# One attention and two mixture layers in one program: the first head's queries in one piece, the weight splits of MoE 1 placed and ordered anew, the weight split of MoE 2 moved behind the second group's rows

## The chip, the core and the metric

The program runs on one core of a Trainium2 chip. The core has a matmul engine (TensorE, PE in the profile, with PEld for its weight loads), a vector engine (VectorE, DVE), an activation engine (ScalarE, ACT), GpSimd (POOL), and SyncE (SP), which here only issues DMAs. Each engine runs its own list of instructions in the order written, and waits at an instruction until what it needs is done. The metric is the device time of one execution in microseconds (us). Before the change it is 1084.62 us, the median of three runs (1084.51 to 1084.77).

## The reference, cut to what matters

```python
# 1. attention: q is pooled by pairs of positions (1152 -> 576), 4 batches of 8 heads, head size 64
q_pool = q.reshape(B, H, S // 2, 2, D).mean(axis=3)
scores = scale * q_pool @ k.T
attn = exp(scores - max(scores)); attn = attn / sum(attn)
x = (attn @ v).transpose(0, 2, 1, 3).reshape(2304, 512)
# 2. MoE 1, in truth one dense layer pair
h = x @ w_in                                   # 512 -> 2048
g = where(h > 0, h, exp(min(h, 0)) - 1)
x = g @ w_out                                  # 2048 -> 512
# 3. MoE 2: a row is skipped or goes to one of 8 experts (512 -> 1024 -> 512)
do = x @ w_skip > 0; e = argmax(x @ w_gate); p = softmax(x @ w_gate)[e]
out = where(do, x + p * (maximum(x @ w1[e], 0) @ w2[e]), x)
```

## The kernel before, in words

A float32 operand that must be multiplied nearly exactly is split: a high part (`hi`, rounded to the fast matmul type by ACT) and a low part (`lo`, the rest, by a subtraction on DVE or POOL). A product then is three matmuls: high by high, high by low, low by high.

**Attention** (lines 25 to 273) goes through 16 pairs of heads. A pair has nine units of 128 queries against 1152 keys (one unit has 64 queries of either head). For a unit PE makes scores in a large piece `s2` (768 keys, two buffers) and a small one `s1` (384 keys, one buffer); DVE finds the maximum (L122, L128, L130), ACT takes the exponential (`ex`, L137 and L138) into a tile `p` of the pool `pp` (three buffers), PE transposes `p` in three groups (L165), DVE and ACT copy these out (`PT`, L169, L170), and PE multiplies by v (L180). The order in which a unit's steps are issued is the string `order='TSeTqsdTvr'`. For the very first pair the queries and keys are prepared apart, in `first(j)` (L193 to 210): `hi` and `lo` split the keys, `add` sums the two positions of a query on POOL and DVE (L200), then come the cast `qh` (L205 or L67) and the rest `ql` (L206 or L71). The first head's queries come in two pieces, 256 columns and 320; the second piece's work (`late`, L220) is issued behind the first unit's exponential and the second head's preparation (L243).

**MoE 1** (lines 319 to 404) runs over nine blocks `b` of 256 rows and 16 chunks `f` of 128 inner columns. `stage1(b,f)` is twelve matmuls (L357), then ACT's exponential (L361), two DVE instructions that make `e` (L362, L363; the second one frees the PSUM buffer `ph`, of which there are two), ACT's high part `gh` (L365) and DVE's low part `gl` (L367). `stage2(b,f)` is six matmuls (L375), two chunks behind. In block 0 `load` also brings two weight tiles a chunk (`rawi`, `rawo`, five raw buffers) and splits them on ACT (L337) and DVE (L338) at once. The first split tiles come from the pool `ip`, which takes over memory that the attention's tiles held: a tile there waits until their last readers are done.

**MoE 2** (lines 596 to 794) treats the largest expert's first two groups of rows, "a" and "b", ahead of the rest. Its weights `w1` are used as they are, `w2` is split (L639, L640) into `w2hi`, `w2lo`. `turn` transposes a group's gathered rows `xg` on PE (L646) and copies them out on ACT or DVE (L647, L648) into `xt`; `layer1` is the first product (L656) with its ReLU and split `hh`, `hl` (L658, L659); `second` is the second product (L675): sixteen matmuls with `w2hi`, then eight with `w2lo`, `py`. The group (0,0) follows "b".

Of the kernel before, what the change touches and what calls it, by code (L numbers as in the profile page):

```python
# [11 lines left out]
F32 = mybir.dt.float32  # L12
BF16 = mybir.dt.bfloat16
F32R = mybir.dt.float32r
I32 = mybir.dt.int32
U32 = mybir.dt.uint32
AF = mybir.ActivationFunctionType
ALU = mybir.AluOpType
# [3 lines left out]
P = 128  # L22


def attention(ctx,tc,qT,kT,vt,xT,ident,dram,side=None,init=None,nside=1.25,order='TSeTqsdTvr',evac=(1, 0, 0),LAG=2,TP=3,KB=1,KH=1,VW=6,LW=7,RD=1,V0=0.0,D0=5,PLAN={4: ['k', 'aK'], 5: ['as', 'bK'], 6: ['aq', 'bs', 'aQ'], 7: ['bq', 'bQ', 't']},EX=1,WARM=24):
    nc=tc.nc
    B,H,D,S=kT.shape
    SQ=S//2; NC=S//P
    SC=1.0/16.0
    pp=ctx.enter_context(tc.tile_pool(name="pp",bufs=LAG+1))  # L30
    kp=ctx.enter_context(tc.tile_pool(name="kp",bufs=2))
# [16 lines left out]
    def load_q(pr,j):  # L48
        b,hp=divmod(pr,H//2)
        qr=state[pr]["qr"][j]=kp.tile([P,2,SQ],F32,tag=f"qr{j}",name=f"qr{pr}_{j}",bufs=1)  # L50
        src=qT[b,2*hp+j].rearrange("f d n -> d f n")
        for c in ((slice(0,256),slice(256,SQ)) if pr==j==0 else (slice(0,SQ),)):
            for r in range(2): nc.sync.dma_start(qr[r*64:r*64+64,:,c],src[:,:,c])
    def load_v(pr):
        b,hp=divmod(pr,H//2)
        for j in range(2):
# [42 lines left out]
    NU=len(units)  # L99
    S3=S//3  # L100
# [31 lines left out]
    def ex(i):  # L132
        d=cur[i]; nm=d["nm"]; key,_,n=place(d["u"])
        if key not in sums: sums[key]=sp.tile([P,5,2],F32,tag="a2",name="a2_%d_%d"%key)
        a2=sums[key]
        pt=pp.tile([P,S],F32,tag="p",name="p"+nm)
        nc.scalar.activation(pt[:,2*S3:],d["s1"][:,0,:S3],AF.Exp,bias=d["nb"],scale=SC,accum_out=a2[:,n,1:2])  # L137
        nc.scalar.activation(pt[:,:2*S3].rearrange("p (c s) -> p c s",c=2),d["s2"][:,:,:S3],AF.Exp,bias=d["nb"],scale=SC,accum_out=a2[:,n,0:1])  # L138
        d["pt"]=pt
# [47 lines left out]
    V=nc.vector; G=nc.gpsimd  # L187
# [5 lines left out]
    def first(j):  # L193
        st=state[0]; r=slice(64*j,64*j+64); o=slice(64-64*j,128-64*j); ks=st["ks"][j]; kr=st["kr"]
        def hi(x,y): nc.scalar.activation(ks[r,x:y],kr[r,x:y],AF.Copy)
        def lo(x,y): V.tensor_tensor(out=ks[o,x:y],in0=kr[r,x:y],in1=ks[r,x:y].bitcast(F32),op=ALU.subtract)
        def add(c=slice(0,SQ)):
            qs=st["qs"][j]=st["qs"][j] or kp.tile([P,SQ],F32,tag=f"qs{j}",name=f"qs0_{j}",bufs=1)
            for h,e in ((slice(0,64),G),(slice(64,128),(V,G)[j])):
                e.tensor_tensor(out=qs[h,c],in0=st["qr"][j][h,0,c],in1=st["qr"][j][h,1,c],op=ALU.add)  # L200
        if j==0:

            qh=st["qh"][0]=kp.tile([P,SQ],F32R,tag="qh0",name="qh0_0"); ql=st["ql"][0]=kp.tile([P,SQ],F32R,tag="ql0",name="ql0_0")
            def q(c):
                add(c); nc.scalar.activation(qh[:,c],st["qs"][0][:,c],AF.Copy)  # L205
                V.tensor_tensor(out=ql[:,c],in0=st["qs"][0][:,c],in1=qh[:,c].bitcast(F32),op=ALU.subtract)  # L206
            hi(0,2*S3); lo(0,2*S3); q(slice(0,256)); hi(2*S3,S); lo(2*S3,S)
            return lambda: q(slice(256,SQ))
        else:
            hi(0,S); add(); lo(0,S); q_hi(0,j); q_lo(0,j,G)  # L210
    def others():
        for j in range(2):
            r=slice(64*j,64*j+64); o=slice(64-64*j,128-64*j)
            copy(state[0]["kh"],state[0]["ks"][j],r); copy(state[0]["kl"],state[0]["ks"][j],o)
        q_tail(0)
        load_v(0)
        load_k(1); load_q(1,0); load_q(1,1)
        if side: side.pop(0)()
        if init: init()
    late=first(0)  # L220
    PL={"as":lambda p:q_sum(p,0,G),"bs":lambda p:q_sum(p,1,G),"k":k_hi,"t":q_tail,"aq":lambda p:q_hi(p,0),"bq":lambda p:q_hi(p,1),
        "aK":lambda p:k_lo(p,0,G),"bK":lambda p:k_lo(p,1,G),"aQ":lambda p:q_lo(p,0,G),"bQ":lambda p:q_lo(p,1,G)}
    last={(u[0],u[1]//2):i for i,u in enumerate(units) if u[1] in (1,3) and u[2]==1}
# [2 lines left out]
    for i in range(NU+LAG+8):  # L226
        k=i-LAG; w=i%9
        nxt=i<NU and units[i][0]+1<NPR
        pr=i//9
        if nxt:  # L230
            if pr+2<NPR:
                if w==LW: load_k(pr+2)
                if w==LW+1: load_q(pr+2,0)
        if w==0 and 1<=pr and pr+1<NPR and i<NU: load_q(pr+1,1)
        if nxt:
            if w==VW: load_v(pr+1)
        credit+=rate
        nv=min(len(pend),int(credit)) if i<NU else len(pend)
        credit-=nv
        nvs=order.count("v"); g=0; vi=0  # L240
        for o in order:
            if o=="r" and i==0:
                ex(0); first(1); late(); others()  # L243
            if o=="S":
                if i<NU: s_big(i)
            elif o=="e":
                if 1<=i-EX<NU: ex(i-EX)
                while kept: kept.pop(0)()
            elif o=="q":
                while after: after.pop(0)()  # L250
                if nxt:
                    for x in PLAN.get(w,()): PL[x](pr+1)
            elif o=="s":
                if i<NU: s_small(i)
            elif o=="v":
                for _ in range((nv*(vi+1)+nvs-1)//nvs-(nv*vi+nvs-1)//nvs):
                    if pend: pend.pop(0)()
                vi+=1
            elif o=="T":
                if 0<=k<NU: transpose(k,g)  # L260
                g+=1
            elif o=="r":
                if i-RD in ends: rinv(ends[i-RD])
            elif o=="d":
                if side and D0<=i<NU:
                    sc+=nside
                    while sc>=1 and side: side.pop(0)(); sc-=1
        if 0<=k<NU:
            cur.pop(k)
            if k in ends:  # L270
                assert not pend
                rows(ends[k]); pend+=pv_parts(ends[k]); rate=(9/4 if ends[k][1]==0 else 9/5)+.01; credit=V0
# [46 lines left out]
def moe1(ctx,tc,xp,rp,xT,w_in,w_out,on_pair,R,TB=256,LAGF=2,raw=None,XF=(13,6),EXTRA=(3,5,7,9,11,13)):  # L319
    nc=tc.nc  # L320
# [3 lines left out]
    ip=ctx.enter_context(tc.tile_pool(name="ip",bufs=1))  # L324
    wp=ctx.enter_context(tc.tile_pool(name="wp",bufs=1))
    gp=ctx.enter_context(tc.tile_pool(name="gp",bufs=3))
    psH=ctx.enter_context(tc.tile_pool(name="psH",bufs=2,space=PSUM))
    psX=ctx.enter_context(tc.tile_pool(name="psX",bufs=2*NTT,space=PSUM))
    wih=[];wil=[];woh=[];wol=[]
    wi_v=w_in.rearrange("(k p) f -> p k f",p=P); wo_v=w_out.rearrange("(k p) e -> p k e",p=P)  # L330
    def load(kind,f):
        shape=[P,KC,P] if kind=="i" else [P,DM]
        r=rp.tile(shape,F32,tag="raw",name=f"raw{kind}{f}")
        pool=ip if f<(3 if kind=="i" else 1) else wp
        hi=pool.tile(shape,F32R,name=f"w{kind}h{f}"); lo=pool.tile(shape,F32R,name=f"w{kind}l{f}")
        nc.sync.dma_start(r,wi_v[:,:,f*P:(f+1)*P] if kind=="i" else wo_v[:,f])
        nc.scalar.activation(hi,r,AF.Copy)  # L337
        nc.vector.tensor_tensor(out=lo,in0=r,in1=hi.bitcast(F32),op=ALU.subtract)  # L338
        (wih if kind=="i" else woh).append(hi); (wil if kind=="i" else wol).append(lo)
    xs={}  # L340
    def xsplit(b):
# [8 lines left out]
    def stage1(b,f):  # L350
        xh,xl=xs[b]
        ph=psH.tile([P,512],F32,tag="ph",name=f"ph{b}_{f}")
        wh,wl=wih[f],wil[f]
        n=0
        for cc in range(KC):
            for w,x in ((wh,xh),(wh,xl),(wl,xh)):
                nc.tensor.matmul(ph[:,:TB],w[:,cc],x[:,cc],start=(n==0),stop=(n==3*KC-1)); n+=1  # L357
        if b==0 and f+2<KF: load("i",f+2)
        if b==0 and f+1<KF: load("o",f+1)
        e=gp.tile([P,TB],F32,tag="e",name=f"e{b}_{f}",bufs=2)  # L360
        nc.scalar.activation(e,ph[:,:TB],AF.Exp)  # L361
        nc.vector.tensor_scalar(out=e,in0=e,scalar1=1.0,scalar2=-1.0,op0=ALU.min,op1=ALU.add)  # L362
        nc.vector.scalar_tensor_tensor(out=e,in0=ph[:,:TB],scalar=0.0,in1=e,op0=ALU.max,op1=ALU.add)  # L363
        gh=gp.tile([P,TB],F32R,tag="gh",name=f"gh{b}_{f}"); gl=gp.tile([P,TB],F32R,tag="gl",name=f"gl{b}_{f}")
        nc.scalar.activation(gh,e,AF.Copy)  # L365
        mid()
        nc.vector.tensor_tensor(out=gl,in0=e,in1=gh.bitcast(F32),op=ALU.subtract)  # L367
        G[(b,f)]=(gh,gl)
# [17 lines left out]
    q=[]; todo=[]; mids=[]  # L386
    def mid():
        if mids and next(mids[0])=="after": todo.append(mids.pop(0))
# [207 lines left out]
class Experts:  # L596
# [117 lines left out]
    def run(s,steps,psL):  # L714
        tc,nc,r=s.tc,s.nc,s.r; E=r.E
        with ExitStack() as c:
# [4 lines left out]
            for _ in range(3):  # L721
                next(steps); next(la)
            next(steps)
            s.split(0,"hi")
            for _ in la: pass
            s.turn("b",3,"b",e=nc.vector)
            next(lb)
            for _ in steps:
                next(lb); next(lb)
# [12 lines left out]
            def turn(k,j,e=None):  # L742
                x=s.at[k,j]=len(s.at)%4; s.turn((k,j),x,f"{k}_{j}",e=e)
            i=2
# [13 lines left out]
                    next(fews[k])  # L758
                return go
            s.layer2(0,s.lta[:,0],"a","a",ha,0)  # L760
            turn(0,0)
            s.layer2(0,s.lta[:,1],"b","b",hb,1)
            tile(0,0,{7:[lambda: turn(0,1)]})
            tile(0,1,{7:[lambda: (turn(3,0),turn(1,2,nc.vector))]},{1:[lambda: turn(1,0)]})
            s.load(4,ee[4])
# [108 lines left out]
```

## Time and profile before

| what | value |
|---|---|
| median of three runs | 1084.62 us |
| the profiled execution | 1084.87 us, its span 1083.2 us |
| PE busy | 1044.2 us, 96% of the span |
| DVE, ACT, POOL busy | 738.6, 589.0, 320.0 us |
| mean granted TensorE clock | 0.991 of 2.4 GHz |

The profiled execution lasts 1.67 us longer than its span. Its time is within 0.25 us of the median. A timeline row is: start in us, duration in us, engine, source line, operation, what is written and read, how many instructions are merged (xN); in brackets the idle time of the engine just before the row, and what ended it.

### The profile page before, as it was taken

To read this page: it belongs to the slowest core of one execution; us is meant where nothing else is said; L and a number is where in the kernel's file an instruction comes from. 1 tells how busy PE (TensorE), PEld (TensorE's weight loads), DVE (VectorE), ACT (ScalarE), POOL (GpSimd) and SP (SyncE) were. 2 spreads that over 40 slices of the span, in tenths; PEclk is the share of its full clock that TensorE was granted. 3 is DMA by queue.
4 is the path that set the end of the run, shared out by engine and by line. 5 is a ranking of instruction groups with operands and counts; after the bars stand their busy time and mean duration, and the time that the engine had idled before them with its cause. 6 is when DMAs were issued, how large, how long until landed. Compare 5 with 4: busy or idle time off the path is not lost. (4 is left out here: it accounts for less than half of the span.)

```text
span 1083.2 us, 20229 instructions
## 1 busy us (share of the span) xinstructions
PE 1044.2 (96%) x7435; PEld 852.5 (79%) x7435; DVE 738.6 (68%) x1887; ACT 589.0 (54%) x1365; POOL 320.0 (30%) x500
## 2 busy tenths in 40 slices
PE   6999999999999999999999999999999999999995
PEld 5677776777767766777688999999999998888884
DVE  4788877887878887876577646778777675542331
ACT  4888787887778877887554323333333333220230
POOL 4565445666445665443000000000000000114111
PEclk8999999999999999999999999999999999999998
DMA  8765556765566664553074010110101101338960
GB/s 209 197 166 161 145 152 168 190 188 145 152 157 178 190 177 137 153 145 95 4 201 145 22 40 21 40 39 2 40 1 40 38 3 40 110 106 307 400 221 11
DMA packets 66156, 133.56 MB, mean 123 GB/s; under 512 B 9212, under 2 KB 18940, under 8 KB 66048
## 3 DMA queue, kind: packets, MB, share of 16 engines
q1 hardware_dynamic: 63904, 127.44, 40.0%
q0 software_dynamic: 2144, 4.75, 1.4%
q8 instruction: 60, 0.98, 0.4%
q14 instruction: 48, 0.39, 0.1%
HBM read 93.37 MB, written 20.17 MB: 105 GB/s over the span
## 5 line engine op out<-in xcount | busy, mean ns | idle before, releaser
L165 PE MATMUL t<-ident,p 128*128 128x128 f32 x1152 | 197.5, 281 | 8.5 <-ACT PT L170 7.9
L165 PEld LDWEIGHTS t<-ident,p 128*128 128x128 f32 x1152 | 137.7, 141 | 70.0 <-ACT PT L170 27.9
L170 ACT ACTIVATE PT<-t 128x384 f32<-128x384 f32 x288 | 140.0, 492 | 62.2 <-PE t L165 58.1
L180 PE MATMUL o<-PT,v 128*64 128x256 f32 (+1 forms) x1152 | 170.3, 418 | 0.0
L357 PE MATMUL ph<-xh,wih 128*128 128x256 f32 x576 | 163.4, 284 | 2.0 <-DVE e L363 1.2
L357 PE MATMUL ph<-xl,wih 128*128 128x256 f32 x576 | 162.1, 282 | 0.0
L357 PE MATMUL ph<-xh,wil 128*128 128x256 f32 x576 | 161.1, 280 | 0.2 <-DVE wil L338 0.2
L534 POOL DMA_INDIRECT rowlist<-meta,sl x18 | 18.8, 1042 | 431.9 <-DVE sl L533 248.7
L115 PE MATMUL s<-ks,qh 128*128 128x384 f32 x384 | 130.5, 394 | 8.9 <-ACT p L137 5.3
L122 DVE TENSOR_REDUCE m<-s 128x1 f32<-128x768 f32 x128 | 122.4, 956 | 15.7
L365 ACT ACTIVATE gh<-e 128x256 fp32r<-128x256 f32 x144 | 60.2, 418 | 130.6 <-DVE e L363 130.6
L85 POOL TENSOR_TENSOR kl<-kr,kh 64x288 fp32r<-64x288 f32 x120 | 97.1, 839 | 96.8 <-ACT kh L81 89.8
L361 ACT ACTIVATE e<-ph 128x256 f32<-128x256 f32 x144 | 55.0, 382 | 129.5 <-PE ph L357 129.5
L357 PEld LDWEIGHTS ph<-xh,wih 128*128 128x128 f32 x576 | 108.2, 188 | 12.8 <-issue 6.0
L138 ACT ACTIVATE p<-s,nb 128x768 f32<-128x768 f32 x128 | 115.1, 899 | 0.0
L375 PE MATMUL px<-woh,gh 128*128 128x512 f32 x288 | 114.9, 399 | 0.0
L169 DVE COPY PT<-t 128x384 f32<-128x384 f32 x144 | 79.5, 552 | 51.1 <-PE t L165 49.4
L375 PE MATMUL px<-wol,gh 128*128 128x512 f32 x288 | 113.6, 395 | 0.0
L180 PEld LDWEIGHTS o<-PT,v 128*64 128x64 f32 x1152 | 70.3, 136 | 53.3 <-issue 22.3
L357 PEld LDWEIGHTS ph<-xl,wih 128*128 128x128 f32 x576 | 108.3, 188 | 5.0
L375 PE MATMUL px<-woh,gl 128*128 128x512 f32 x288 | 112.2, 389 | 0.0
L115 PE MATMUL s<-ks,ql 128*128 128x384 f32 x384 | 109.4, 339 | 0.0
(258 smaller groups left out, 1943.0 us busy)
## 6 DMA issues: line engine op xcount, KB each, us to landing
qr<-qT SPq DMA_DIRECT2D x62, 288.0 KB, 7.6
w<-w SPq DMA_DIRECT2D x16, 1024.0 KB, 13.8
v<-vt SPq DMA_DIRECT2D x32, 288.0 KB, 3.3
kr<-kT SPq DMA_DIRECT2D x15, 576.0 KB, 6.5
ks<-kh SPq DMA_DIRECT2D x30, 288.0 KB, 3.9
ks<-kl SPq DMA_DIRECT2D x30, 288.0 KB, 3.4
d<-w_in SPq DMA_DIRECT2D x16, 512.0 KB, 5.2
d<-w_out SPq DMA_DIRECT2D x16, 512.0 KB, 4.2
```

The source lines that it names most:

```text
L85: for c in range(0,S,S//4): e.tensor_tensor(out=st["kl"][o,c:c+S//4],in0=st["kr"][r,c:c+S//4],in1=st["kh"][r,c:c+S//4].bitcast(F32),op=ALU ...
L115: nc.tensor.matmul(dst[:,ci,:S3],st[n][j][:,t*P:t*P+P],st["ks"][j][:,c*S3:c*S3+S3],start=first,stop=last)
L122: nc.vector.tensor_reduce(out=m2[:,0:1],in_=s2[:,:,:S3],op=ALU.max,axis=AX.XY)
L138: nc.scalar.activation(pt[:,:2*S3].rearrange("p (c s) -> p c s",c=2),d["s2"][:,:,:S3],AF.Exp,bias=d["nb"],scale=SC,accum_out=a2[:,n,0:1])
L165: nc.tensor.transpose(po[:,c],pt[:,(g*3+c)*P:(g*3+c+1)*P],ident)
L169: if evac[g]: nc.vector.tensor_copy(o,s)
L170: else: nc.scalar.activation(o,s,AF.Copy)
L180: nc.tensor.matmul(cell["o"][64*a:64*a+64,:n],state[pr]["v"][a][:,c],src[:,c,a,:n],start=(c==0),stop=(c==NC-1))
L357: nc.tensor.matmul(ph[:,:TB],w[:,cc],x[:,cc],start=(n==0),stop=(n==3*KC-1)); n+=1
L361: nc.scalar.activation(e,ph[:,:TB],AF.Exp)
L365: nc.scalar.activation(gh,e,AF.Copy)
L375: nc.tensor.matmul(X[b][t][:,:DM],a[:,t*P:(t+1)*P],w,start=(f==0 and i==0),stop=(f==KF-1 and i==2))
```

## The change

Lines of the changed program are numbered some 2 to 10 lower than those of before, since lines went away.

```diff
     def load_q(pr,j):
-        src=qT[b,2*hp+j].rearrange("f d n -> d f n")
-        for c in ((slice(0,256),slice(256,SQ)) if pr==j==0 else (slice(0,SQ),)):
-            for r in range(2): nc.sync.dma_start(qr[r*64:r*64+64,:,c],src[:,:,c])
+        for r in range(2): nc.sync.dma_start(qr[r*64:r*64+64],qT[b,2*hp+j].rearrange("f d n -> d f n"))
...
-            hi(0,2*S3); lo(0,2*S3); q(slice(0,256)); hi(2*S3,S); lo(2*S3,S)
-            return lambda: q(slice(256,SQ))
+            hi(0,2*S3); lo(0,2*S3); hi(2*S3,S); add(); q_hi(0,j); q_lo(0,j,V); lo(2*S3,S)
...
-            if o=="r" and i==0:
-                ex(0); first(1); late(); others()
+            if o=="r" and i==0: first(1); others()
...
-                if 1<=i-EX<NU: ex(i-EX)
+                if 0<=i-EX<NU: ex(i-EX)
...
-        pool=ip if f<(3 if kind=="i" else 1) else wp
+        pool=ip if f<(2 if kind=="i" else 1) else wp
...
         nc.scalar.activation(hi,r,AF.Copy)
-        nc.vector.tensor_tensor(out=lo,in0=r,in1=hi.bitcast(F32),op=ALU.subtract)
+        def low(): nc.vector.tensor_tensor(out=lo,in0=r,in1=hi.bitcast(F32),op=ALU.subtract)
+        if kind=="i" or f==0: low()
+        else: lows.append(low)
...
         nc.scalar.activation(gh,e,AF.Copy)
+        while lows: lows.pop(0)()
...
+            for _ in la: pass
+            s.turn("b",3,"b")
             s.split(0,"hi")
-            for _ in la: pass
-            s.turn("b",3,"b",e=nc.vector)
...
-            turn(0,0)
-            s.layer2(0,s.lta[:,1],"b","b",hb,1)
+            for n,_ in enumerate(s.second(0,s.lta[:,1],"b","b",hb,1)):
+                if n: turn(0,0)
```

Where the instructions stand now is shown by three pieces of the built programs. At the program's start on ACT, before (`ks` are the first pair's keys, `qh` the queries' high parts of head 0 and 1, `p` the exponentials, `s` the scores):

```order
L195 ACTIVATE ks_0_155<-kr_116 64x768
L205 ACTIVATE qh_0_157<-qs_0_161 128x256
L195 ACTIVATE ks_0_155<-kr_116 64x384
L137 ACTIVATE p_0_0_182,a_0_0_181<-s_0_0_175,nb_0_0_179 128x384
L138 ACTIVATE p_0_0_182,a_0_0_181<-s_0_0_168,nb_0_0_179 128x768
L195 ACTIVATE ks_1_156<-kr_116 64x1152
L67 ACTIVATE qh_1_190<-qs_1_186 128x576
L205 ACTIVATE qh_0_157<-qs_0_161 128x320
L137 ACTIVATE p_1_0_303,a_0_0_181<-s_1_0_284,nb_1_0_288 128x384
```

And in the changed program:

```order
L193 ACTIVATE ks_0_153<-kr_116 64x768
L193 ACTIVATE ks_0_153<-kr_116 64x384
L65 ACTIVATE qh_0_161<-qs_0_158 128x576
L193 ACTIVATE ks_1_154<-kr_116 64x1152
L65 ACTIVATE qh_1_185<-qs_1_181 128x576
L135 ACTIVATE p_0_0_276,a_0_0_275<-s_0_0_174,nb_0_0_178 128x384
L136 ACTIVATE p_0_0_276,a_0_0_275<-s_0_0_167,nb_0_0_178 128x768
L135 ACTIVATE p_1_0_298,a_0_0_275<-s_1_0_279,nb_1_0_283 128x384
```

The first unit's exponential stands behind both heads' casts now, and the second unit's exponential right behind it, where the late piece of head 0 stood.

On DVE from the last product of the attention into MoE 1's first chunks, before (`xT` is that product, `wil` and `wol` are low parts of weights, `e` and `gl` those of the chunk's inner values):

```order
L185 TENSOR_TENSOR xT<-o_1_6989,bc_1_6987 128x256
L338 TENSOR_TENSOR wil_7054<-rawi_7052,wih_7053 128x512
L338 TENSOR_TENSOR wil_7060<-rawi_7058,wih_7059 128x512
L338 TENSOR_TENSOR wol_7066<-rawo_7064,woh_7065 128x512
L338 TENSOR_TENSOR wil_7085<-rawi_7083,wih_7084 128x512
L338 TENSOR_TENSOR wol_7091<-rawo_7089,woh_7090 128x512
L362 TENSOR_SCALAR e_0_7095<-e_0_7095 128x256
L363 SCALAR_TENSOR_TENSOR e_0_7095<-ph_0_7070,e_0_7095 128x256
L367 TENSOR_TENSOR gl_0_7100<-e_0_7095,gh_0_7099 128x256
```

And in the changed program:

```order
L329 TENSOR_TENSOR wil_7049<-rawi_7047,wih_7048 128x512
L329 TENSOR_TENSOR wil_7055<-rawi_7053,wih_7054 128x512
L329 TENSOR_TENSOR wol_7061<-rawo_7059,woh_7060 128x512
L183 TENSOR_TENSOR xT<-o_1_6984,bc_1_6982 128x256
L329 TENSOR_TENSOR wil_7080<-rawi_7078,wih_7079 128x512
L355 TENSOR_SCALAR e_0_7089<-e_0_7089 128x256
L356 SCALAR_TENSOR_TENSOR e_0_7089<-ph_0_7065,e_0_7089 128x256
L329 TENSOR_TENSOR wol_7086<-rawo_7084,woh_7085 128x512
L361 TENSOR_TENSOR gl_0_7094<-e_0_7089,gh_0_7093 128x256
```

Three splits went ahead of the attention's last product, and the `wol` of each chunk from ahead of the two instructions on `e` to behind them, ahead of `gl`.

On ACT in MoE 2, before (`ex` belongs to the router, `hha` and `hhb` are the inner values of groups "a" and "b", `pt` holds transposed rows):

```order
L504 ACTIVATE ex_11999<-d_11993 128x16
L639 ACTIVATE w2hi_11907<-xT 128x2048
L639 ACTIVATE w2hi_11908<-xT 128x2048
L658 ACTIVATE hha<-pha_11963 128x512
L658 ACTIVATE hha<-pha_12026 128x512
L658 ACTIVATE hhb<-phb_12053 128x512
```

And in the changed program:

```order
L498 ACTIVATE ex_11994<-d_11988 128x16
L652 ACTIVATE hha<-pha_11958 128x512
L652 ACTIVATE hha<-pha_12019 128x512
L642 ACTIVATE xt_11898<-ptb 128x512
L633 ACTIVATE w2hi_11902<-xT 128x2048
L633 ACTIVATE w2hi_11903<-xT 128x2048
L652 ACTIVATE hhb<-phb_12048 128x512
```

The two wide splits moved behind group "a"'s inner values and group "b"'s transposed rows, whose copy was on DVE. On PE the four transpositions of group (0,0) moved from ahead of group "b"'s second product to behind its sixteenth matmul.

## Rows read from the trace of the kernel before

**Rows 1.** Busy time by stretches: us, then engines; last granted clock, DMA, GB/s
```profile
15.88:26.12 10.24, 6.41 (x25) 5.71 (x24) 5.65 (x10) 4.83 (x12) 6.41 (x53) 0.50 1.03 272
30.00:530.00 500.00, 490.99 (x3550) 363.44 (x3550) 394.57 (x824) 401.50 (x950) 262.54 (x394) 1.00 0.57 155
590.00:952.00 362.00, 361.82 (x2350) 327.37 (x2349) 246.08 (x858) 115.02 (x279) 17.93 (x18) 1.00 0.11 39
```

**Rows 2.** Timeline of the first 22 us, from the first unit's exponential on
```profile
10.38 2.87 POOL L200 TENSOR_TENSOR qs<-qr 64x576 f32<-64x576 f32 x2 [4.41 <-DMA qr<-qT]
10.68 0.58 ACT L137 ACTIVATE p<-s,nb 128x384 f32<-128x384 f32 x1 [2.52 <-DVE nb L130]
...
11.40 0.44 PE L115 MATMUL s<-ks,qh 128*128 128x384 f32 x1 [1.24 <-ACT p L137]
...
13.44 0.68 ACT L67 ACTIVATE qh<-qs 128x576 fp32r<-128x576 f32 x1
...
14.20 2.27 POOL L71 TENSOR_TENSOR ql<-qs,qh 128x288 fp32r<-128x288 f32 x2 [0.95 <-ACT qh L67]
...
14.84 0.98 DVE L200 TENSOR_TENSOR qs<-qr 64x320 f32<-64x320 f32 x1
...
17.82 0.49 DVE L206 TENSOR_TENSOR ql<-qs,qh 128x320 fp32r<-128x320 f32 x1 [2.00 <-ACT qh L205]
...
19.10 0.55 DVE L128 TENSOR_REDUCE m<-s 128x1 f32<-128x384 f32 x1
...
20.71 0.69 PE L115 MATMUL s<-ks,qh 128*128 128x384 f32 x1 [3.83 <-ACT p L137]
```

**Rows 3.** Timeline from the attention's end into MoE 1's first chunks
```profile
538.70 1.15 ACT L337 ACTIVATE wih<-rawi 128x512 fp32r<-128x512 f32 x2 [3.62 <-PE o L180]
...
539.38 0.38 PE L357 MATMUL ph<-xh,wih 128*128 128x256 f32 x1 [0.85 <-ACT wih L337]
...
543.27 0.36 PE L357 MATMUL ph<-xh,wih 128*128 128x256 f32 x1 [0.30 <-DVE e L363]
```

**Rows 4.** Timeline of one late chunk of block 0, from `gh` on
```profile
578.72 0.42 ACT L365 ACTIVATE gh<-e 128x256 fp32r<-128x256 f32 x1 [1.23 <-DVE e L363]
...
580.09 0.36 ACT L361 ACTIVATE e<-ph 128x256 f32<-128x256 f32 x1
...
580.31 0.68 DVE L338 TENSOR_TENSOR wol<-rawo,woh 128x512 fp32r<-128x512 f32 x1
...
580.91 0.28 DVE L362 TENSOR_SCALAR e<-e 128x256 f32<-128x256 f32 x1
...
581.80 0.36 PE L357 MATMUL ph<-xh,wih 128*128 128x256 f32 x1
```

**Rows 5.** Timeline of PE: first chunk of block 1, and two later chunks
```profile
585.72 0.36 PE L357 MATMUL ph<-xh,wih 128*128 128x256 f32 x1 [0.89 <-DVE e L363]
...
591.42 0.28 PE L357 MATMUL ph<-xh,wih 128*128 128x256 f32 x1
...
594.22 0.28 PE L357 MATMUL ph<-xh,wih 128*128 128x256 f32 x1
```

**Rows 6.** Timeline of MoE 2's groups "a" and "b"
```profile
958.39 3.70 ACT L639 ACTIVATE w2hi<-xT 128x2048 fp32r<-128x2048 f32 x2
...
962.22 0.60 PE L646 MATMUL ptb<-ident,xgb 128*128 128x128 f32 x4
...
963.80 0.68 DVE L647 COPY xt<-ptb 128x512 f32<-128x512 f32 x1
...
964.54 1.16 PE L656 MATMUL phb<-xt,xT 128*128 128x128 f32 x8 [1.72 <-DVE xt L647]
...
979.59 0.66 PE L646 MATMUL pt<-ident,xg 128*128 128x128 f32 x4 [1.56 <-DMA xg<-x2d,lt]
...
980.35 0.60 ACT L648 ACTIVATE xt<-pt 128x512 f32<-128x512 f32 x1 [7.26 <-PE pt L646]
...
983.81 2.03 PE L675 MATMUL pyb<-w2lo,hhb 128*128 128x512 f32 x8
```

More of the change, by code (lines that the diff above doesn't have):

```diff
@@ L196, in lo, with add @@
         def lo(x,y): V.tensor_tensor(out=ks[o,x:y],in0=kr[r,x:y],in1=ks[r,x:y].bitcast(F32),op=ALU.subtract)
-        def add(c=slice(0,SQ)):
-            qs=st["qs"][j]=st["qs"][j] or kp.tile([P,SQ],F32,tag=f"qs{j}",name=f"qs0_{j}",bufs=1)
+        def add():
+            qs=st["qs"][j]=kp.tile([P,SQ],F32,tag=f"qs{j}",name=f"qs0_{j}",bufs=1)
             for h,e in ((slice(0,64),G),(slice(64,128),(V,G)[j])):
-                e.tensor_tensor(out=qs[h,c],in0=st["qr"][j][h,0,c],in1=st["qr"][j][h,1,c],op=ALU.add)
+                e.tensor_tensor(out=qs[h],in0=st["qr"][j][h,0],in1=st["qr"][j][h,1],op=ALU.add)
         if j==0:
[L203 to L206, printed above, removed]
-            hi(0,2*S3); lo(0,2*S3); q(slice(0,256)); hi(2*S3,S); lo(2*S3,S)
-            return lambda: q(slice(256,SQ))
+            hi(0,2*S3); lo(0,2*S3); hi(2*S3,S); add(); q_hi(0,j); q_lo(0,j,V); lo(2*S3,S)
         else:
@@ L219, in others @@
         if init: init()
-    late=first(0)
+    first(0)
     PL={"as":lambda p:q_sum(p,0,G),"bs":lambda p:q_sum(p,1,G),"k":k_hi,"t":q_tail,"aq":lambda p:q_hi(p,0),"bq":lambda p:q_hi(p,1),
@@ L328, in moe1 @@
     psX=ctx.enter_context(tc.tile_pool(name="psX",bufs=2*NTT,space=PSUM))
-    wih=[];wil=[];woh=[];wol=[]
+    wih=[];wil=[];woh=[];wol=[];lows=[]
     wi_v=w_in.rearrange("(k p) f -> p k f",p=P); wo_v=w_out.rearrange("(k p) e -> p k e",p=P)
```

## The prediction

> **What bounds the kernel now.** I read the busy times by stretches first. In the attention PE is busy 490.99 of 500 us, in MoE 1 after its first block 361.82 of 362 [rows 1]: there nothing but PE's own work counts, and no part of the change takes a matmul away. So I went to the places where PE stands idle, and read each with the engine named as the one that ended the wait. Three of them touch the change. At the start PE waits 3.83 us for an exponential [rows 2]; from the attention's end through block 0 of MoE 1 it waits again and again for ACT and DVE [rows 3 to 5]; at MoE 2's beginning it waits 1.72 us for a copy and 1.56 us for gathered rows [rows 6]. Behind each place PE is the bound again, so what PE wins or loses there should reach the end. An idle time of another engine, such as ACT's 7.26 us [rows 6], is worth nothing by itself.
>
> **Part 1, the start.** Before, the second unit's maximum on DVE (19.10) stands behind `ql` of head 0's late piece (17.82), for which DVE waited 2.00 us: `ql` needs the cast `qh`, that the addition on POOL, and POOL did head 1's `ql` first (14.20, 2.27 us) [rows 2]. With one piece this chain is gone. What is late next is the first unit's exponential, now behind both casts. POOL's additions for head 1 end at 10.38 + 2.87 = 13.25; the cast begins at 13.44 and takes 0.68, so the exponential begins at 14.12 in place of 10.68, 3.44 later. PE's next scores followed it by 11.40 − 10.68 = 0.72: 14.84. They take 0.44; the maximum can follow at once, at about 15.3, and from a maximum to the scores that waited for its exponential it was 20.71 − 19.10 = 1.61: these can start at 16.9 in place of 20.71. But PE has the third unit's products and two groups of transpositions to do between. Before, its list from 11.40 was done at 20.71 − 3.83 = 16.88, that is in 5.48 us with the waits in it; with all of that they start at 20.3, so between 16.9 and 20.3. I take the middle, 18.6: 2.1 us earlier. That stretch runs at a granted clock of 0.50, up to 26.12 [rows 1]. If the clock rises at the same time as before, the work done early is worth half, 1.05; if it rises as much earlier, all 2.1. I take **−1.5**.
>
> The bounds: at best the whole idle time goes, −3.8. At worst the wait only moves to another place and the larger additions come on top. One of 64x576 takes POOL 2.87 / 2 = 1.44, which PE then loses at half clock (0.7) or in full: about +1.0. What hides them: POOL stood idle 4.41 us ahead of head 1's additions, waiting for the load [rows 2]; without that cover they cost the 1.44. SP issues two loads fewer, POOL one addition fewer, and `others` comes a little earlier; I cost these at nothing, beside the loads.
>
> The addition of 320 columns on DVE at 14.84, while POOL's subtraction ran, took 0.98 us; DVE's subtraction of as many columns at 17.82, with POOL silent, took 0.49 [rows 2]. The Trainium skill ("SBUF — State Buffer", section "SBUF: two separate sides") says that DVE, with two operands from SBUF, and GpSimd, reading SBUF, take turns at one port pair and the loser blocks for a whole instruction. The pair of rows agrees. By it head 0's two additions, now of 576 columns, would run one behind the other, and if the first scores are on the path they come later by the shorter one, about 0.49 x 576 / 320 = 0.88; at half clock that is 0.44, the start −1.1 and the whole 1076.1. I keep the sum above, since the first exponential now waits for the casts and not for these scores.
>
> **Part 2, MoE 1.** First its beginning. PE waits 0.85 us for `wih`, the first high part, and ACT had waited 3.62 us for the attention's last product [rows 3]: not for the data, but for the memory. In the changed order three DVE splits stand ahead of that product's normalisation, since the first tiles now take the exponentials' memory, which is free once the last transpositions are done; ACT's 3.62 us have room for the three casts of about 0.6 and DVE had nothing to do there either. Then PE goes on at 539.38 − 0.85 = 538.53. The third chunk started at 543.27. It can't before two chunks' first products are done, 2.80 us (a period of 2.80 in a later block [rows 5] is a `stage1` and a `stage2`, with as many columns each): 541.3; the second weight pair still comes late, I take 541.5, **−1.75**. The bounds of this step: −0.85 (only the first wait goes) and −1.95.
>
> Then the chunks of block 0. From the third chunk to the sixteenth it was (581.80 − 543.27) / 13 = 2.964 us each [rows 3, 4], though PE needs 2.80 [rows 5]. The row of chunk 15 shows a ring over ACT and DVE: the exponential is done at 580.45, but DVE is in `wol` (580.31, 0.68 us) and takes the minimum at 580.91 [rows 4]. In the changed order `wol` stands behind the two instructions on `e`. It gives back up to 580.91 − 580.31 = 0.60 from the ring, which then takes 2.37, less than 2.80. A second ring, `gh` to exponential (580.09 − 578.72 = 1.37), exponential to minimum (0.36 and about 0.05 for the hand-over) and minimum to the next `gh` (578.72 + 2.964 − 580.91 = 0.78) is 2.56, still below. So PE's 2.80 sets the period: 13 x 0.164 = 2.1 less, and chunk 15 starts at 541.5 + 13 x 2.80 = 577.9. At block 1, PE waited 0.89 and the first chunk came 585.72 − 581.80 = 3.92 after the last one [rows 4, 5]; with DVE no longer behind, 2.80: 580.7. That is 585.72 − 580.7 = 5.0 in all; I take **−4.9**. Bounds: −1.7 (the period and the wait at block 1 stay) and −5.0.
>
> What could use it up: `gl` comes 0.68 later in each chunk, behind `wol`, but its matmuls stand two chunks behind. A raw buffer is freed later by about 0.9, so the loads come later; the five of them cover that, as no row of the stretch has PE, ACT or DVE waiting for such a load. If they didn't, the period would stay near 2.96, which is the lower bound.
>
> **Part 3, MoE 2.** Before, ACT is in the two `w2hi` splits from 958.39 to 962.09, then makes group "a"'s inner values, and DVE copies group "b"'s rows at 963.80, 1.58 after PE transposed them (962.22). PE waits 1.72 [rows 6]. Now ACT copies them itself, with the splits behind. Where ACT did such a copy without a queue ahead, it began 980.35 − 979.59 = 0.76 after the transposition and took 0.60; with 0.06 for the hand-over, as from DVE's copy to PE (964.54 − 963.80 − 0.68), PE starts at 962.22 + 1.42 = 963.64: **−0.9**. The splits then end 3.70 after about 963.4, at 967.1; they are read by the second products, behind group "b"'s first one, sixty-four matmuls of which eight take about 1.1, so not ahead of some 8 us after 963.64: nothing is late. Then the transposition of group (0,0) waited 1.56 for gathered rows. It goes behind sixteen matmuls, which took about 983.81 − 979.59 − 0.60 = 3.6: the rows are there, and its copy on ACT lies beside the eight `w2lo` products of 2.03 [rows 6]. **−1.56**. The bounds are −0.9 and −2.5: if the gather comes later with the router it still has 3.6 − 1.56 = 2.0 to spare. The loads of the later experts start with PE's own progress and are hidden as before.
>
> **Sum.** 1.5 + 4.9 + 2.5 = 8.9. The profiled execution took 1084.87, 0.25 over the median: 1084.87 − 8.9 = 1075.97, and against the median **1075.7**.
>
> **The rivals.**
> *Block 0 stays as it is.* Another ring over ACT and DVE, the raw loads, or memory that is not free as early as I read from the order keep the period at 2.96 and the wait at block 1. For it: DVE's own list in a chunk does not get shorter (two splits of 0.68 and three smaller instructions, the shown one 0.28 [rows 4]). Against it: both rings are shorter by the rows. Then MoE 1 gives 1.75 alone: 1084.6 − 5.75 = 1078.9.
> *The start gains nothing.* The exponential, 3.44 later, may cost what the late piece gave. Then 1077.2, with a loss of 1.0 1078.2.
> *The low clock lasts longer.* The granted clock stayed at 0.50 up to 26.12, in a stretch in which PE was busy 6.41 of 10.24 us [rows 1]. After the change PE stands idle longer ahead of 15, with fewer scores done before the first exponential. If the stretch at 0.50 is as long once more, the work of 10.24 us at half clock costs 5.1 us: 1080.8. If it comes back three times, 15.4 is lost against 8.9: about 1091, slower than before. The point from which it decides is 17.8 us more at half clock. Against it: from 15 on PE waits less than before.
> The Trainium skill ("TensorE: Matmul & The Clock Gate", section "Part 1: The HAM clock gate") has the array throttled by default and released by activity. By this rule longer first waits mean a longer throttled stretch, so the 1080.8; the rise at 26.12, after PE's waits had ended, agrees with it, and no row shows how much idling it bears.
>
> **How the numbers follow.** The forecast has 0.66, block 0 as it is 0.12, the start without gain 0.15, the low clock once more 0.05, more than that 0.02. The forecast's own spread is 1.5 either way, from the start's bounds. The range is 1073.9 to 1079.0: it takes in the forecast and the first two rivals, and leaves out about 2 in 10, with both of them together. About 0.2%, 2.2 us, is what a measurement of this kernel can tell from no change: faster holds in all cases but the last and some unforeseen, 0.93; 0.04 for the same, 0.03 for slower.
>
> **What would show it.** In the profile of the changed kernel: the scores that started at 20.71 start near 18.6, and the granted clock is 1.00 from about 26; MoE 1's first matmul stands right behind the attention's last one; a chunk of block 0 takes 2.80 and no 0.89 stands at block 1; group "b"'s first product comes 1.4 behind its transposition; group (0,0)'s transposition waits for no load. The forecast is wrong if PE's idle time at these places is only moved, above all if it turns up as a wait for `e` or for `wil` in block 0.

## The result and the profile after

The changed kernel takes 1073.25 us (1072.68 to 1074.24, five runs) against 1084.51 (1083.30 to 1084.77) before: a ratio of 0.990 with a 95% interval of 0.9886 to 0.9915, some 11.3 us less. Forecast were 1075.7, and 1073.9 to 1079.0 as the range: the direction was right, the gain 2.4 larger and 0.65 outside the range. The profiled execution took 1073.66, its span is 1071.9 (1083.2 before).

Three events tell where the 11.2 between the two spans went: the start of the attention's last matmul (the last of its last product with v, `o`) moved from 538.14 to 534.79 (3.35: the start), that of MoE 1's last matmul, seen from there, from 414.38 to 409.46 later (4.92: MoE 1), and that of PE's last matmul of all, from there, from 117.49 to 114.76 (2.73: MoE 2). The rest, 0.2, lies in the last scatter.

The start first, as a timeline of the changed kernel (columns as in [rows 2]):

```profile
9.40 0.76 PE L113 MATMUL s<-ks,qh 128*128 128x384 f32 x2 [2.60 <-ACT qh L65]
...
11.96 0.69 PE L113 MATMUL s<-ks,qh 128*128 128x384 f32 x1 [1.06 <-DVE ks L194]
...
13.91 0.58 ACT L135 ACTIVATE p<-s,nb 128x384 f32<-128x384 f32 x1
...
14.64 0.69 PE L113 MATMUL s<-ks,qh 128*128 128x384 f32 x1 [0.38 <-ACT p L135]
...
15.99 0.54 DVE L126 TENSOR_REDUCE m<-s 128x1 f32<-128x384 f32 x1
...
17.99 0.67 PE L113 MATMUL s<-ks,qh 128*128 128x384 f32 x1
...
22.50 0.59 PE L113 MATMUL s<-ks,qh 128*128 128x384 f32 x2
```

the scores that answer to the last row in the kernel before:

```profile
26.81 0.59 PE L115 MATMUL s<-ks,qh 128*128 128x384 f32 x2
```

and the changed kernel's busy time by stretches (columns as in [rows 1]), cut where the granted clock changed:

```profile
6.30:9.71 3.41, 0.81 (x7) 0.56 (x5) 1.81 (x3) 1.02 (x2) 1.64 (x1) 1.00 1.01 224
9.71:19.95 10.24, 8.79 (x31) 7.02 (x29) 8.99 (x14) 5.34 (x12) 8.49 (x33) 0.50 0.78 196
19.95:30.00 10.05, 9.16 (x59) 7.62 (x57) 6.66 (x12) 9.58 (x24) 5.53 (x28) 1.00 1.02 261
```

The first exponential starts at 13.91 (forecast 14.12), the scores that had waited 3.83 us start at 17.99 (18.6; before 20.71) without any wait. PE's waits of the first 20 us now all lie ahead of 14.64, the last of them short (0.38), and the stretch at 0.50 of the clock (1.2 GHz), the slow stretch from here on, lies at 9.71 to 19.95, no longer at 15.88 to 26.12.

MoE 1's beginning, on all three engines, and the first products of chunks 3 and 15 of block 0 and of chunk 0 of block 1 (answering to [rows 3 to 5]):

```profile
531.13 0.62 ACT L328 ACTIVATE wih<-rawi 128x512 fp32r<-128x512 f32 x1
...
531.78 1.49 DVE L329 TENSOR_TENSOR wil<-rawi,wih 128x512 fp32r<-128x512 f32 x2 [1.41 <-ACT wih L328]
...
535.11 0.39 PE L350 MATMUL ph<-xh,wih 128*128 128x256 f32 x1
...
541.03 0.28 PE L350 MATMUL ph<-xh,wih 128*128 128x256 f32 x1
...
574.71 0.28 PE L350 MATMUL ph<-xh,wih 128*128 128x256 f32 x1
...
577.51 0.28 PE L350 MATMUL ph<-xh,wih 128*128 128x256 f32 x1
```

The casts lie in ACT's former idle time, PE's row has no bracket (it did not wait), the twelve periods from chunk 3 at 541.03 to chunk 15 at 574.71 took 2.807 each, and block 1 follows after 2.80.

MoE 2 (answering to [rows 6]):

```profile
953.95 0.60 PE L640 MATMUL ptb<-ident,xgb 128*128 128x128 f32 x4
954.64 0.60 ACT L642 ACTIVATE xt<-ptb 128x512 f32<-128x512 f32 x1
955.14 3.70 ACT L633 ACTIVATE w2hi<-xT 128x2048 fp32r<-128x2048 f32 x2
...
955.29 1.16 PE L650 MATMUL phb<-xt,xT 128*128 128x128 f32 x8 [0.75 <-ACT xt L642]
...
972.38 0.60 PE L640 MATMUL pt<-ident,xg 128*128 128x128 f32 x4
972.74 2.10 PE L669 MATMUL pyb<-w2lo,hhb 128*128 128x512 f32 x8
```

Group "b"'s product starts 1.34 behind its transposition (2.32 before), and `pt` waits for no load.

### The profile page after: what moved, and what is told of

It reads as the page before. It is cut to its first block, busy times and chain, and to the rows that moved or that the text cites. A ratio compares the mean times of both kernels' runs of the same rounds, so it can differ in the third digit from the quotient of the medians.

```text
span 1071.9 us, 20208 instructions
## 1 busy us (share of the span) xinstructions
PE 1041.6 (97%) x7435; PEld 854.5 (80%) x7435; DVE 740.7 (69%) x1885; ACT 589.9 (55%) x1365; POOL 319.8 (30%) x499
## 5 line engine op out<-in xcount | busy, mean ns | idle before, releaser
L120 DVE TENSOR_REDUCE m<-s 128x1 f32<-128x768 f32 x128 | 122.4, 957 | 15.8 <-PE s L113 0.5
```

Source lines behind the costliest of these rows:

```text
L120: nc.vector.tensor_reduce(out=m2[:,0:1],in_=s2[:,:,:S3],op=ALU.max,axis=AX.XY)
```

## The experiments

The runs were made in sets, each on one chip beside the kernel before; the median of before stands in brackets. Edits are to the kernel before or to the changed one, as the first line of each diff says.

**The three parts alone, and the change without its first part.** The diffs are the pieces of the change shown above.

e1_start_only: 

> The kernel before with part 1 alone (head 0's queries in one piece, the first exponential behind both casts). Theory A, the start itself is worth what the two traces show at the attention's end: 538.53 - 535.11 = 3.4 us less than before, about 1081.1, and the stretch at a granted clock of 0.50 ends near 20 as in the changed kernel. Theory B, the change's traced execution had its slow stretch at a lucky place, and the start is worth the 1.5 of the prediction: about 1083.0, with the slow stretch ending anywhere between 16 and 27. Theory C, the whole start gain is a moved wait: no change, 1084.5.

1080.97 (1084.9), ratio 0.9968 (0.9956 to 0.9980). Six runs from 1080.37 to 1083.72. The start alone gives 3.9, as theory A had it; the slow stretch ends at 17.82. The longest of the six runs has no trace.

e2_moe1_only: 

> The kernel before with part 2 alone (MoE 1's first tiles in the exponentials' memory, the low parts of w_out behind e). Forecast of the prediction and reading of the two traces: 4.9 us less, about 1079.6; MoE 1's first matmul right behind the attention's last one (538.5), block 1 about 4.9 earlier than 585.72. Rival: the start of the changed kernel shifted loads and so helped MoE 1; then this is under 4 less, over 1080.5.

1080.53 (1084.9), ratio 0.9964 (0.9953 to 0.9976): 4.4 less by the medians, seven runs from 1079.36 to 1082.47. In its trace MoE 1 is 4.94 shorter, as in the changed kernel; nothing of it needs the start.

e3_moe2_only: 

> The kernel before with part 3 alone (w2's wide splits behind group b's rows, group (0,0)'s transposition behind sixteen matmuls). Reading of the two traces: PE's last product 2.7 earlier and up to 0.3 from the end: 2.7 to 3.0 less, about 1081.7. Rival, the prediction's sum: 2.5 less, 1082.0. If the gathers come late without the earlier parts: 0.9 less, 1083.6, with a wait for xg left.

1083.41 (1084.9), ratio 0.9986 (0.9977 to 0.9995): only 1.5, less than any of its cases with both waits gone. The wait for the rows went and the one for the copy fell from 1.72 to 0.7, but a new one came: group (0,0)'s first product took 8.64 to the next transposition, 7.14 before the change. This is called the stall below.

e4_no_start: 

> The changed kernel with part 1 undone (parts 2 and 3 only). Theory A (the start is worth 3.4): 1073.25 + 3.4 = 1076.7. Theory B (1.5, and the rest is the place of the slow stretch in one execution): 1074.8 to 1075.2. If the parts add up, its gain is that of the MoE 1 part and of the MoE 2 part together, 7.6 to 7.9 less than before. Its trace is one more sample of the old start: where the granted clock falls and rises.

1078.53 (1084.9), ratio 0.9938 (0.9925 to 0.9952): 6.4 less, longer than either theory. Its trace has the same stall (8.80, that is 1.66); with that added back the parts give 8.0, near the 7.6 to 7.9 expected.

**What the start's gain is made of.** The edits change the warm-up; e5 is the changed kernel once more:

```diff
 # changed kernel (e6, e8) or the kernel before (e7)
-WARM=24
+WARM=48   # e6, e7
+WARM=8    # e8
```

e5_after_again: 

> The changed kernel once more, for another sample of its start and its ratio on the chip of the other three. Theory A (the start part's size is set by where the stretch at a granted clock of 0.50 lies): the stretch falls before 12 and rises before 21 again, since PE now waits longest ahead of its first scores, and the attention's last product starts within 0.5 of 534.8 or 533.9, as the rise is near 19.95 or 17.82. Theory B (chance): the stretch lies anywhere, also at 16 to 26 as in three of the four traces with the old start, with the time 2 to 3 us longer.

e6_after_warm48: 

> The changed kernel with 48 warm-up matmuls in place of 24, which fill PE's idle 2.6 us ahead of the first scores. Theory A: with PE busy there the clock falls later, in the waits from 11 on, and rises later (after 22), so that more of the attention's work lies in the slow stretch: 1 to 3 us longer than the changed kernel; or it does not fall at all, and it is 2 to 4 us shorter. Theory B (only the order of the work counts): within 0.5 of the changed kernel, as the first scores start when their operands come.

e7_before_warm48: 

> The kernel before with 48 warm-up matmuls. They end about 1.3 us after its first scores could start. Theory A: the slow stretch moves or goes, and the attention's end with it, by more than 0.6. Theory B: PE has 3.8 us of idle time behind, so the later first scores cost nothing: within 0.5 of before.

e8_after_warm8: 

> The changed kernel with 8 warm-up matmuls. Theory A: PE is idle for longer ahead of its first scores, so the slow stretch lies still earlier, or the clock is at 0.50 from the start and is released by the first scores, before 19: up to 1 shorter, or as long, and the attention's last product before 534.8. Theory B: within 0.5 of the changed kernel.

Medians 1074.62, 1074.43, 1086.06 and 1074.88 (1084.69); e7's ratio is 1.0011 (1.0002 to 1.0020). What the traces of all kernels show at the start (waits of PE over 0.35 in its first 25 us, the slow stretch, and the start of the attention's last matmul):

| kernel | PE's last wait ends | clock at 0.50 | attention's last matmul |
|---|---|---|---|
| before; e2, e4 | 20.7 in all three | 15.8 to 26.1 in all three | 538.14; 538.16, 538.19 |
| e3, e9, e10, e11, e16 (old start) | 20.4 to 20.9 | to 23.70, 24.38, 23.59, 24.34, 23.88 | 537.02, 537.40, 536.99, 537.44, 537.02 |
| e7 (old start) | 22.73 | 14.72 to 28.38 | 540.37 |
| changed; e5, e14, e12 | 14.64; 14.50, 14.44, 14.67 | to 19.95; 20.23, 19.65, 20.33 | 534.79; 534.16, 534.60, 534.09 |
| e1 | 14.69 | 10.99 to 17.82 | 533.92 |
| e6 | 14.46 | 14.07 to 17.48 | 533.13 |
| e8 | 14.49 | to 20.82 | 535.06 |
| e15, e17, e18 (see below) | 14.43, 14.54, 14.73 | to 18.26 (and again later), 20.07, 20.39 | 537.23, 536.41, 536.55 |

With the old start the last column follows the end of the slow stretch: 538.14 − 536.99 = 1.15 for 26.12 − 23.59 = 2.53, nearly the half that half a clock makes. (The trace of e8 notes the clock from 20.82 on; ahead of that two matmuls of scores take 0.84, as in the slow stretches, and behind it 0.52.) e7 is 1.4 longer, against its theory B, but in it the first scores come later as well as the waits, so it does not tell the two apart. For e6 and e8 the medians lie within 0.5 of e5, as theory B said; only the single traces differ, by 1.0 and 0.9. Theory A's own forecasts failed there too: in e6 the slow stretch became shorter and ended earlier, with the first scores later (9.64), and in e8 the clock rose at 20.82, not before 19. So these two decide nothing.

The test with the old order, in which the wait alone is filled:

```diff
 # kernel before, s_big(i)
-        smm(u,s2,(0,1))
+        for _ in range(4 if i==2 else 1): smm(u,s2,(0,1))
```

e13_before_busy: 

> The kernel before, in which PE computes the third unit's large scores four times (the same values into the same place), which fills most of its 3.8 us wait ahead of 20.71 and adds nothing else. Theory A (the clock's rise follows the end of PE's last long wait): that wait now ends near 15, the clock rises before 22 in place of 23.6 to 26.1, and the attention's last product starts 1.5 to 3 us earlier (about 535.5), the whole about 1082. Theory B (the start's gain is the earlier order of work itself): the chain over POOL, ACT and DVE is unchanged, so the time stays within 0.4 of before, or is longer by up to 0.5.

1082.51 (1084.21), ratio 0.9987 (0.9978 to 0.9996), with more work on PE. The third unit's scores with the repeats, and the scores that waited 3.83 us in the kernel before:

```profile
14.91 0.98 PE L115 MATMUL s<-ks,qh 128*128 128x384 f32 x2 [2.12 <-DVE ks L196]
...
20.69 0.62 PE L115 MATMUL s<-ks,qh 128*128 128x384 f32 x1
```

Its stretches:

```profile
14.27:21.09 6.82, 6.18 (x20) 5.93 (x21) 4.66 (x8) 1.60 (x4) 5.83 (x23) 0.50 0.89 230
21.09:30.00 8.91, 8.20 (x52) 6.79 (x52) 6.93 (x13) 8.42 (x21) 3.67 (x36) 1.00 1.05 276
```

PE's last long wait ends at 14.91, the clock rises at 21.09, and the last matmul of the attention starts at 536.23, 1.9 earlier than in the trace of before and 0.8 than in that of e16, on the same chip with the rise at 23.88. The scores that waited in the kernel before start at 20.69, there at 20.71: nothing is computed sooner up to that point. So an earlier end of the waits alone is worth 1.7 us by the medians: theory A, at the lower end of what it expected.

**Halves of the parts.** e9 moves w2's splits and the copy, e10 the transposition of (0,0), e11 the low parts, each on the kernel before.

e9_moe2_copy: 

> The kernel before with the first half of part 3 alone: w2's wide splits behind group b's rows, which ACT copies. Reading of the traces: 0.97 less (PE starts group b's product 0.75 instead of 1.72 after a wait), 1083.7. If this half brings the new stall in group (0,0)'s first product (1.5 to 1.6, seen in five of six traces with part 3 and in none without it): 0.6 more than before, 1085.3, and the product takes 8.6 to 8.8 from its start to the next transposition.

e10_moe2_turn: 

> The kernel before with the second half of part 3 alone: group (0,0)'s transposition behind sixteen matmuls of group b's second product. Reading of the traces: the wait of 1.56 goes and 1.7 less at PE's last matmul, 1083.0. If this half brings the new stall: 0.1 to 0.2 less, 1084.5, with group (0,0)'s first product 8.6 to 8.8 long in place of 7.14.

e11_moe1_low: 

> The kernel before with the second half of part 2 alone: the low parts of w_out behind e, without the exponentials' memory. The prediction's step: block 0's chunks take 2.80 in place of 2.96, the wait at block 1 goes, MoE 1 starts as before, so 4.9 - 1.75 = 3.2 less, 1081.5, with block 1 at 582.5. Rival: the rings over ACT and DVE recover only because the chunks began earlier: under 1.5 less.

1083.15, 1082.44 and 1080.29 (1084.13); ratios 0.9992 (0.9983 to 1.0001), 0.9984 (0.9975 to 0.9993), 0.9967 (0.9955 to 0.9980). The halves of part 3 give 1.0 (an interval that just reaches no change) and 1.7, and neither trace has the stall on this chip. The low parts alone shorten MoE 1 by 3.53 in the trace; that leaves 1.4 for the memory, which was not run alone.

**The stall in group (0,0).** A gather is a load of single rows by their numbers, issued by POOL (`bring`). The edit moves four of them:

```diff
 # changed kernel, run()
-            for k,j in ((1,2),(1,1),(4,0),(2,0),(5,0)): bring(k,j)
+            bring(1,2)
...
             tile(0,0,{7:[lambda: turn(0,1)]})
+            for k,j in ((1,1),(4,0),(2,0),(5,0)): bring(k,j)
```

e12_gathers_late: 

> The changed kernel with four of the five gathers that run beside group (0,0)'s first product moved behind that group. Theory S (the stall there, 1.5 to 1.6, comes from the gathers running beside the weight loads): the product takes 7.1 to 7.3, 1.4 less than the changed kernel on the same kind of chip (1074.6), 1073.2. Rival (the stall is tied to the order of PE's work, or to the loads alone): 8.6 to 8.8 as before, 1074.6. If the later gathers are needed too early: a wait for xg on PE, over 1075.

e14_after3: 

> The changed kernel a third time, as the neighbour of the other two on this chip: 0.9895 to 0.9905 of before. If its group (0,0)'s first product takes 7.14, this chip does not show the stall; if 8.6 to 8.8, it does.

e15_gathers_late2: 

> The changed kernel with four gathers behind group (0,0), once more. Theory S (the stall comes from the gathers beside the loads): 7.14 for group (0,0)'s first product whatever the chip, 1.4 to 1.6 less than the changed kernel where that shows the stall, the same where it does not. Theory C (the stall goes with the chip or the place of the buffers): as long as the changed kernel here, either way.

e16_moe2_turn2: 

> The kernel before with the second half of part 3 alone, once more. Without the stall 1.7 less than before; where the changed kernel shows the stall here and this one does too, 0.1 to 0.2 less, and the moved transposition brings it; where only the changed kernel shows it, it needs the earlier copy as well.

e12: 1073.46 (1084.13). On the chip of the other three: 1073.38, 1072.92 and 1082.37 (1084.21). No kernel shows the stall on these two chips (on e12's the whole change was not run with the gathers in their old place), so e12 and e15 tell nothing of its cause; on e15's chip the later gathers cost nothing. The traces of e5, e6 and e8 had it (8.67 to 8.76), all on a third chip, those of e3 and e4 on a fourth. On the third and the fourth the product is a little longer without part 3 as well: 7.28 in e7, 7.69 and 7.68 in e1 and e2. So part 3 makes larger what these chips show without it.

e15's profiled run took 1076.16, its others 1072.72 to 1073.00, and its trace shows why: a side task on DVE, the integer work on `w_in`, waited for its load, PE waited behind it, and the clock fell a second time (timeline, then a stretch):

```profile
31.74 1.06 DVE L287 TENSOR_SCALAR da<-d 128x512 int32<-128x512 int32 x1 [3.90 <-DMA d<-w_in]
...
33.85 1.33 PE L153 MATMUL r<-ident,ri 128*64 128x128 f32 x12 [3.44 <-DVE ri L144]
```
```profile
31.91:38.74 6.83, 4.89 (x26) 4.61 (x27) 5.68 (x12) 2.64 (x7) 4.78 (x6) 0.50 1.00 227
```

The same task in the changed kernel, with a wait of PE behind it, and then in the kernel before, where the load was there:

```profile
30.27 0.89 DVE L287 TENSOR_SCALAR da<-d 128x512 int32<-128x512 int32 x1 [1.70 <-DMA d<-w_in]
...
34.93 0.55 PE L163 MATMUL t<-ident,p 128*128 128x128 f32 x3 [0.78 <-DVE PT L167]
```
```profile
32.77 1.03 DVE L296 TENSOR_SCALAR da<-d 128x512 int32<-128x512 int32 x1
```

So the task was moved:

```diff
 # e17: the changed kernel; e18: with the later gathers as well
-D0=5
+D0=6
```

e17_after_side_later: 

> The changed kernel with the side task (the integer work on w_in) beginning one unit later. If DVE's wait for that load is what the start gives back: the wait goes, PE's wait of 1.07 at 32.2 shrinks to under 0.95 and the 0.78 behind it goes, 0.5 to 1.0 less than the changed kernel, about 1072.6, and no run over 1075. Rival: PE waits there for ACT's copies as before the change, and the task's instructions only come later: no change, 1073.4.

e18_side_and_gathers: 

> The changed kernel with the side task one unit later and four gathers behind group (0,0). As e17, and on a chip that shows the stall in group (0,0)'s first product 1.5 less still; on one that does not, the same as e17, 1072.6, within 0.4.

1076.77 and 1074.82 (1084.45); ratios 0.9928 (0.9914 to 0.9941) and 0.9913 (0.9900 to 0.9927). The wait for the load went, and at first that gave what was expected: in e17 the scores that start at 39.14 in the changed kernel (42.47 in the kernel before) start at 37.75, so it is 4.72 ahead of the kernel before where the changed kernel is 3.33 ahead. But the task now falls on other units in all of the attention: between 57 and 82 us PE waits 1.4 for ACT's copies, in the changed kernel not at all, and the attention's last matmul starts at 536.41: a miss, 1.6 worse than without the edit. The pair is worth more for the stall, which this chip shows. e17, then e18, group (0,0)'s first product:

```profile
976.20 4.18 PE L650 MATMUL ph<-xt,xT 128*128 128x128 f32 x36
980.99 0.49 PE L650 MATMUL ph<-xt,xT 128*128 128x128 f32 x3 [0.61 <-issue]
981.71 0.37 PE L650 MATMUL ph<-xt,xT 128*128 128x128 f32 x1 [0.23 <-issue]
982.42 2.94 PE L650 MATMUL ph<-xt,xT 128*128 128x128 f32 x24 [0.34 <-issue]
982.62 0.60 ACT L652 ACTIVATE hh<-ph 128x512 fp32r<-128x512 f32 x1 [7.49 <-remote]
...
985.19 0.60 PE L640 MATMUL pt<-ident,xg 128*128 128x128 f32 x4
```
```profile
976.34 7.31 PE L650 MATMUL ph<-xt,xT 128*128 128x128 f32 x64
980.11 0.60 ACT L652 ACTIVATE hh<-ph 128x512 fp32r<-128x512 f32 x1 [4.83 <-PE ph L650]
983.48 0.60 PE L640 MATMUL pt<-ident,xg 128*128 128x128 f32 x4
```

On one chip, with the place of the gathers as the only edit, the product takes 8.99 or 7.14, and the medians differ by 1.95: moving the gathers takes the stall away. The edit moves something else with them: POOL's scatter of finished rows, which stands behind the gathers in POOL's list, is issued at 979.77 in e17, just ahead of the stall, and at 974.92 in e18, ahead of the product. So gathers and scatter are not told apart. Why some chips show the stall and what PE waits for ("issue": nothing that the profile shows) stays open.

## Why the prediction was wrong, step by step

**The start, forecast 1.5, was 3.35 in the trace and 3.9 alone (e1): the step that failed is its term for the clock.** The working of the waits held: the late piece's chain is gone, the exponential starts at 13.91 (14.12), and the scores at 17.99 (18.6), 2.7 earlier in place of 2.1. Mis-sized was the sentence on the clock: "If the clock rises at the same time as before, the work done early is worth half, 1.05; if it rises as much earlier, all 2.1." I took the rise to move with these scores or not at all, and expected it at about 26. It came at 19.95, 26.12 − 19.95 = 6.17 earlier. Work done 2.72 earlier at half clock is worth half, 1.36; a slow stretch that ends 6.17 earlier is worth about half of that, 3.1. Together this is 4.4, and behind the slow stretch the changed kernel is 26.81 − 22.50 = 4.31 ahead; some 1.0 of it is given back soon after (below).

The rise moved about as far as the end of PE's last wait, 20.71 − 14.64 = 6.07: between 14.64 and 17.99 PE now has work where it stood idle, at half clock but busy. That the two agree so closely is luck: the trace of before has the latest rise of the old start (23.59 to 26.12 in eight traces), and with the new one the rise lies at 17.48 to 20.82 in ten. That the two ranges do not meet is not luck, and e13 shows the cause apart from the order of the work. The Trainium skill ("TensorE: Matmul & The Clock Gate", section "Part 1: The HAM clock gate") has the clock released by activity; I had used it for the rival with a longer slow stretch alone, and it spoke as well for an earlier end. e13 agrees with it: with PE busy in its wait the clock rises at 21.09, without at 23.59 or later. Why the rise comes just where it does in one execution stays open. The rival itself did not come: the slow stretch is as long as before, 10.24, and earlier. The upper bound of this term, 3.8, held in the changed kernel's trace and not in e1 (3.9; 4.2 in its trace); the range did not go as far.

A part of the start's gain is given back near 32, by a load that the prediction had put at nothing. It expected the loads of `others` a little earlier; that of `w_in` was issued at 20.59 (20.05 before), while DVE came to it 4.2 earlier and waited 1.70. Where DVE waited 1.66 to 2.22 for it (the changed kernel, e1, e8, e14), PE's wait of some 0.78 for DVE's copy is there; where it waited 0.60 to 1.48 (e5, e6, e12), it is not. In e17, with no wait for the load, nothing is given back at this place. The same wait, with the second fall of the clock in e15, is the third rival in small: seen once in a profile, and one more run each of e1 and e12 is as long, without a trace.

The aside on two additions that take turns rests on a row that was misread: at 17.82 POOL was not silent, as its own row in the kernel before says:

```profile
17.85 0.85 POOL L93 CAST qd<-qh 64x64 fp32r<-64x64 f32 x2 [0.56 <-ACT qh L205]
```

The first scores did come later, at 9.40 (7.80 before), but the first exponential waited for head 1's cast (done at 13.89), as the prediction had it, so this cost did not enter the sum. There was little to spare: its other operand, `nb`, was done at 13.81.

**MoE 1, forecast 4.9, was 4.92.** The first wait is gone, the period went from 2.964 to 2.807, the wait at block 1 is gone. The third chunk was 3.05 behind the first (538.16 − 535.11) where I had 2.97. The low parts alone give 3.5, which leaves 1.4 for the memory; I had 3.2 and 1.7. By the medians part 2 alone gives 4.4 (e2). The rival that block 0 stays as it is falls.

**MoE 2, forecast 2.5, was 2.73 in the profiled run.** The copy gave 0.97 (0.9), the moved transposition 1.76 (1.56). Most of this 0.2 is how the idle time is counted: it starts at the recorded end of the last matmul, while eight `w2lo` products that take 2.03 are followed by the next matmul 1.87 after their start where nothing waits (966.78 and 968.65 in the changed kernel). What I did not see is that group (0,0)'s first product may stall for 1.5 to 1.85; where it does, the part is worth 1.5 (e3), and the changed kernel takes 1074.6 (e5), within the forecast range. That run is no success of the forecast: there the loss by the stall hides most of what the start gave above it. The profiled run of the changed kernel doesn't have it.

**Sum.** 3.35 + 4.92 + 2.73 + 0.2 = 11.2, against 8.9: 1.85 of the difference is the start, 0.23 MoE 2, 0.2 the last scatter.

A version that may be better still is the changed kernel with the later gathers: 1072.92 beside 1073.38 on a chip without the stall (no difference that these runs can tell), and 1.95 less on one that shows it, there with the side task moved in both. Beside the changed kernel itself it was not run on such a chip.

## What to carry to other kernels

Where PE runs at half clock, ask when its waits end, and not only how much earlier the work that waited comes: here filling (e13) or removing the last long wait moved the rise of the clock, and each microsecond of that was worth about half a microsecond at the end of the attention (1.15 for 2.53). When a stretch is made earlier, look for the load in it that does not get earlier. One profiled execution shows one place of the slow stretch and may miss a stall that others have; where terms of one or two microseconds count, read several.

## What was not expected of the hardware

With the old start the slow stretch ended at 23.59 to 26.12 from one execution to the next, with the new one at 17.48 to 20.82. It lasted 10.24 in most, but 3.41 in e6, 6.83 in e1, 6.82 in e13 and 13.66 in e7. And PE can lose 1.5 to 1.85 us in the middle of 64 matmuls with no releaser that the profile shows, while ACT, whose next instruction reads these products, comes 2.65 late (6.42 behind the product's start in e17, 3.77 in e18). This went when gathers, and with them a scatter, were moved away from a stretch with large loads.
